# Where the value loads stand in the GpSimd queue of a fused attention and mixer kernel, and what its planner charges for them

## The chip, the cores and the metric

The kernel runs on one core of a Trainium2 chip. The metric is the time of one execution on the device, in microseconds (us). A core has these engines: TensorE (PE in the profile; its weight loads are PEld), VectorE (DVE), ScalarE (ACT), GpSimd (POOL) and SyncE (SP). SP and POOL also issue the DMAs of this kernel, each in its own queue and in program order; the profile calls the hardware queue of SP q1 and the software queue of POOL q0.

## What is computed

There are two stages: block-sparse attention (MoBA), then a token and channel mixer.

```
# attention: q, k, v are (4 batches, 8 heads, 768, 64)
k_rep = mean of k over blocks of 64 keys                  # 12 blocks
gate  = q @ k_rep^T, future blocks at -1e9
mask  = each query's top 3 blocks and its own block, and causal
x     = softmax(q @ k^T / 8, masked) @ v                  # heads side by side: (4, 768, 512)

# mixer
u   = x + (relu(x^T @ w_tok1) @ w_tok2)^T                 # 768 -> 256 -> 768
out = u + relu(u @ w_ch1) @ w_ch2                         # 512 -> 1536 -> 512
```

## The kernel before, in words

The 32 heads are handled as 16 pairs, i = 0 to 15, four pairs to a batch. The numbers below count pairs.

For each pair, `prepare(i)` (line 714) makes these pieces of work. SP loads k and q in float32 (`load_qk`, issued on line 313, two DMAs of 192 KB each for k and two for q). PE transposes them (line 358; tkl and tql in the profile), ACT copies the result out of PSUM to kt and qt (line 367), and POOL casts them to float16 into KA and QA (line 374; for pair 0 ACT does it, line 379). DVE sums keys by block (line 387), PE makes the gate scores (gps, line 405; for groups of pairs gtp, line 415), DVE picks the top three and builds the bias, PE transposes it (bps, line 493), and DVE puts it under QA (line 499). POOL loads the values (`load_v`, line 320) as float16 into one of six V buffers; pair i uses buffer i mod 6, so its load must come after the attention of pair i - 6.

`attend(i)` (line 791) then does for each head three score products (sps, line 513, with a triangle on line 517 for pair 0), three exponentials on ACT (line 526), the causal triangle on DVE (line 533), the product with V (avp, line 545), and the division on DVE (lines 553 and 564).

The mixer of a batch follows once its four pairs are done: tok (lines 576 and 607, with w_tok1), ups (lines 588 and 621, with w_tok2), and the two channel products c (line 657 with w_ch1 and line 678 with w_ch2). For batch 0 the token part is done one pair at a time (lines 607 and 621). Mixer work of one batch is put between the attention work of later ones. Small products on a zero tile, `dummy` (line 695), stand where PE has nothing else before 46 us of the plan.

The order is not written out by hand. Every piece of work is an `Op` with an engine, planned durations (`occ`, `rec`), a list of things it depends on (`deps`) and a priority. `plan` (line 109) simulates the engines at the time the program is built: again and again it takes the piece that can start first, and among those that can start within 60 ns the one with the lowest priority number. The program is then emitted in that order (lines 949 and 950), so that each engine has one fixed instruction order. What the chip waits for is decided apart from the plan, by the data that instructions share: an instruction waits only if it reads or overwrites something that another makes or still uses. An entry in `deps` with no data behind it moves a piece of work in the order and adds no wait on the chip.

Transfers are planned by `transfers` (line 80): one DMA stream for SP and one for POOL, each in order. A transfer begins 1250 ns (SP) or 1500 ns (POOL) after its issue (line 201), takes `size` ns at full rate, and its data counts as landed 700 ns (SP) or 1200 ns (POOL) later (line 105). While both streams are active, POOL gets the share of the rate that `SHARE` (line 77) names for the size of its transfer, and SP gets the rest. The sizes are 1750 for a k or q load of a pair (line 727), 1350 for a value load (line 752), 3200 for each of the two token weights and 2100 for each of the eight channel weights (line 838).

Two lists on lines 831 to 838 add dependencies by hand:

```python
for i in range(6):
    O["v", i].deps.append(O["tr", "ql", i])
...
for n, (at, f) in enumerate(wq):
    W.append(op("POOL", 700, 0, [O[("cast",) + WAIT[n]]], at, f, size=3200 if n < 2 else 2100))
```

So the value loads of pairs 0 to 5 are planned after the query transposes of their own pair (`tr ql`), those of later pairs only after the attention of pair i - 6, and each weight load after one of the casts named in `WAIT` (line 46). POOL's list begins with four copies of a constant (`indicator`, line 333).

Of the kernel before, what the change touches and what calls it, by code (L numbers as in the profile page):

```python
# [39 lines left out]
def QACT(i):  # L40
# [5 lines left out]
WAIT = [("kt", 3, 1), ("kt", 3, 1), ("qt", 3, 1), ("qt", 3, 1), ("qt", 4, 1), ("qt", 4, 1),  # L46
        ("qt", 5, 1), ("qt", 5, 1), ("qt", 6, 1), ("qt", 6, 1)]
# [26 lines left out]
QUEUES = ("SP", "ACTQ", "POOLQ")  # L74


SHARE = ((3000.0, 0.9), (2000.0, 0.9), (0.0, 0.65))


def transfers(moves):  # L80


    todo = {q: sorted([m for m in moves if (m[1].eng == "POOL") == q], key=lambda m: m[0]) for q in (True, False)}
    left = {id(o): o.size for _, o in moves}
    now, ends = 0.0, {}
    while todo[True] or todo[False]:
        head = {q: v[0] for q, v in todo.items() if v and v[0][0] <= now}
        if not head:
            now = min(v[0][0] for v in todo.values() if v)
            continue  # L90
        rate = {q: 1.0 for q in head}
        if len(head) == 2:
            big = head[True][1].size
            rate[True] = next(r for z, r in SHARE if big >= z)
            rate[False] = 1.0 - rate[True]
        step = min(left[id(o)] / rate[q] for q, (_, o) in head.items())
        for q, v in todo.items():
            if v and q not in head:
                step = min(step, v[0][0] - now)
        now += step  # L100
        for q, (_, o) in head.items():
            left[id(o)] -= step * rate[q]
            if left[id(o)] <= 1e-6:
                todo[q].pop(0)
                ends[o] = now + (1200 if q else 700)
    return ends


def plan(ops, rings, near=60.0):


    free = dict(PE=900.0, ACT=4800.0, DVE=4500.0, POOL=5200.0, SP=750.0, SPO=750.0)
    slots = {name: [(0.0, None)] * n for name, n in rings.items()}
    moves = []
    casts = []
    waiting = {}
    users = {}
    ready = {e: [] for e in free}
    done = {}
    for op in ops:  # L120
        n = 0
        for d in op.deps:
            users.setdefault(id(d), []).append(op)
            n += 1
        waiting[id(op)] = n
        if n == 0:
            ready[op.eng].append(op)

    def finish(op, eng):
        return done[id(op)] + (LAT.get(eng, 33) if op.size == 0 else 60)  # L130

    def buf_free(buf, eng):
        t = 0.0
        for u in buf.users:
            if id(u) not in done:
                return None
            t = max(t, finish(u, eng))
        return t

    order = []  # L140
    left = len(ops)
    while left:
        best = None
        for o in [o for o in ready["PE"] if o.prio == IDLE and free["PE"] > WARM_END]:
            ready["PE"].remove(o)
            done[id(o)] = free["PE"]
            left -= 1
        if not left:
            break
        for e, cand in ready.items():  # L150
            if not cand:
                continue
            lst = []
            if e == "SP":
                if any(x.eng == e and x.prio < min(c.prio for c in cand) for x in ops if id(x) not in done):
                    continue
                cand = [min(cand, key=lambda c: c.prio)]
            for op in cand:
                t = free[e]
                if op.prio == IDLE:  # L160
                    last = slots["av"][0][1]
                    f = 0.0 if last is None else buf_free(last, e)
                    if f is None or f > t:
                        continue
                for d in op.deps:
                    t = max(t, finish(d, e))
                ok = True
                for buf in op.takes:
                    first = None
                    for s, (_, old) in enumerate(slots[buf.ring]):  # L170
                        f = 0.0 if old is None else buf_free(old, e)
                        if f is not None and (first is None or f < first[0]):
                            first = (f, s)
                    if first is None:
                        ok = False
                        break
                    t = max(t, first[0])
                    buf.slot = first[1]
                if ok:
                    lst.append((t, op))  # L180
            if not lst:
                continue
            t0 = min(t for t, _ in lst)
            pick = min((x for x in lst if x[0] <= t0 + near), key=lambda x: (x[1].prio, x[0]))
            if best is None or pick[0] < best[0]:
                best = pick
        assert best is not None, "the plan cannot go on"
        t, op = best
        op.start = t
        for buf in op.takes:  # L190
            slots[buf.ring][buf.slot] = (0.0, buf)
        wait = 0.0
        if op.eng == "POOL" and not op.size:
            casts = [(t, t + op.rec)]
        elif op.two and casts and casts[0][0] <= t < casts[0][1]:
            wait = (casts[0][1] - t) % (450.0 if casts[0][1] - casts[0][0] > 900 else 1e9)
        free[op.eng] = t + op.occ + wait
        if op.eng in ("SP", "SPO"):
            free["SP"] = free["SPO"] = t + op.occ
        if op.size:  # L200
            moves.append((t + (1500 if op.eng == "POOL" else 1250), op))
            for o, d in transfers(moves).items():
                done[id(o)] = max(done.get(id(o), 0.0), d)
            now = min(free.values())
            moves = [(a, o) for a, o in moves if done[id(o)] > now - 2000]
        else:
            done[id(op)] = t + op.rec + wait
        ready[op.eng].remove(op)
        order.append(op)
        left -= 1  # L210
        for u in users.get(id(op), []):
            waiting[id(u)] -= 1
            if waiting[id(u)] == 0:
                ready[u.eng].append(u)
    return order, max(done.values())
# [3 lines left out]
def kernel(  # L219
# [71 lines left out]
    def op(eng, occ, rec, deps, prio, fn, takes=(), size=0):  # L291
        o = Op(eng, occ, rec, deps, prio, fn, takes, size)
        ops.append(o)
        return o
# [403 lines left out]
    O = {}  # L698
# [13 lines left out]
    W = []  # L712
# [115 lines left out]
        for i in G:  # L828
            attend(i)

    for i in range(6):
        O["v", i].deps.append(O["tr", "ql", i])
    own_op.deps.append(O["cast", "qt", 4, 1])
    for x in range(2):
        O["cast", "kt", 0, x].deps.append(O["qt", 0])
    O["ksum", 1].deps.append(O["bias", 0])
    for n, (at, f) in enumerate(wq):
        W.append(op("POOL", 700, 0, [O[("cast",) + WAIT[n]]], at, f, size=3200 if n < 2 else 2100))

    for b in range(B):  # L840
        fill = 1000.0 * (b + 1)
# [5 lines left out]
        if b == 0:  # L847
            for c in range(4):
                bk = Buf("bank")
                at = fill + c  # L850
# [64 lines left out]

    kernel_plan.update(ops=O)
    order, span = plan(ops, RINGS)


# [64 lines left out]
```

## Time and profile before

| what | value |
|---|---|
| median of 8 runs | 270.42 us (268.13 to 272.0) |
| the eight runs | 268.13, 268.33, 268.55, 270.11, 270.74, 270.83, 271.62, 272.0 us |
| profiled execution: own time / span | 271.62 us / 269.5 us |
| PE busy | 261.2 us, 97% of the span |
| DVE, ACT, POOL busy | 157.5, 145.3, 79.9 us |
| mean granted TensorE clock | 0.981 |
| DMA | 28.77 MB moved; q1 (SP) 21.33 MB, q0 (POOL) 7.08 MB |
| a value load, from issue to landing | 6.3 us median (4.0 to 9.5), x16 |
| a token weight load | 7.3 and 8.4 us |
| a k or q load (one DMA of 192 KB) | 5.5 and 5.4 us median, x32 each |

A value load keeps POOL for some 1.0 us while it is issued. The order on POOL in the first 60 us of the profiled execution, by start: value loads at 6.23, 8.17, 16.42, 31.39, 35.75, 39.95, 46.69, 49.40, 52.80 and 57.26 us; token weights at 32.39 and 33.20; pairs of channel weights at 36.79, 50.41 and 58.28; casts of pair 1 from 12.07, of pair 2 from 15.65, of pair 3 from 29.74 and of pair 4 from 45.03 us. By the dependencies above, the load at 35.75 belongs to pair 6 and the one at 39.95 to pair 7 (it waited for pair 1's attention), while those of pairs 4 and 5 are at 46.69 and 52.80.

How to read the table: PE is busy nearly always, but busy time includes the dummies and counts a slow product in full. Whether the time could be shorter is seen from what PE did and at which clock, stage by stage.

### The profile page before, as it was taken

Reading aid. Unit: us, or ns where it says so; the run is one execution under the profiler, and the core shown is the slowest. Engines: PE = TensorE matmul, PEld = TensorE weight load, DVE = VectorE, ACT = ScalarE, POOL = GpSimd, SP = SyncE. Lnnn points to the kernel's source line nnn. Section 1 sums busy time; section 2 is a strip of 40 time slices with the busy share of each in tenths; the row PEclk is TensorE's granted clock in tenths of the full one; section 3 lists DMA queues with packets and bytes.
Section 4 is the critical chain, followed back from the end, with each engine's and each line's share of the span. In section 5 each row is a group of like instructions: output and inputs, shape, how many; then the busy total and the mean of one; then the engine's idle time right before and its main releaser. Section 6 shows DMA issues by size and latency. Waiting matters only on the chain.

```text
span 269.5 us, 5879 instructions
## 1 busy us (share of the span) xinstructions
PE 261.2 (97%) x2322; PEld 170.4 (63%) x2322; DVE 157.5 (58%) x536; ACT 145.3 (54%) x195; POOL 79.9 (30%) x112
## 2 busy tenths in 40 slices
PE   7979999999999999899999999999999999999994
PEld 7967878878577768555655566655455544465443
DVE  4553686889696759987566976475233252333222
ACT  3753598877779985657883599860024400044100
POOL 8581563986742966026620000000000000000000
PEclk9985899999999999999999999999999999999999
DMA  8999699999999999119341000006320017210032
GB/s 171 191 204 219 135 157 201 173 184 197 217 179 146 208 172 125 25 56 168 55 83 43 14 2 2 0 2 124 148 78 2 0 23 174 88 68 0 2 133 100
DMA packets 91322, 28.77 MB, mean 107 GB/s; under 512 B 84896, under 2 KB 87840, under 8 KB 91296
## 3 DMA queue, kind: packets, MB, share of 16 engines
q1 hardware_dynamic: 63232, 21.33, 35.3%
q0 software_dynamic: 28064, 7.08, 27.0%
q8 instruction: 18, 0.29, 0.4%
q14 instruction: 8, 0.07, 0.1%
HBM read 26.83 MB, written 6.29 MB: 123 GB/s over the span
## 4 chain that ended last, share of the span: by engine, by line
PE 88%; DMA 5%; SPq 3%; DVE 1%; issue 1%; ACT 0%; DVEq 0%; ACTq 0%
PE c L657 23%; PE c L678 23%; PE sps L513 14%; PE avp L545 8%; DMA ql<-in_q_dram 5%; PE tql L358 3%; PE ups L588 3%; SPq L313 3%; PE tkl L358 3%; PE tok L576 2%; PE gps L405 2%; PE gtp L415 1%; PE avp L695 1%; PE bps L493 1%; PE tok L607 1%; PE ups L621 1%
## 5 line engine op out<-in xcount | busy, mean ns | idle before, releaser
L526 ACT ACTIVATE e<-sps 128x1024 f16<-128x1024 f32 (+1 forms) x96 | 84.6, 922 | 17.9 <-PE sps L513 11.6
L657 PE MATMUL c<-uT,wc 128*128 128x256 f16 (+1 forms) x384 | 69.1, 326 | 0.0
L678 PE MATMUL c<-wc,h 128*128 128x512 f16 (+2 forms) x300 | 65.6, 371 | 0.0
L667 ACT ACTIVATE h<-c 128x512 f16<-128x512 f32 x48 | 28.8, 600 | 61.7 <-PE c L657 42.5
L513 PE MATMUL sps<-QA,KA 88*128 88x512 f16 (+3 forms) x256 | 51.4, 312 | 0.8 <-ACT e L526 0.7
L657 PEld LDWEIGHTS <-wc 128*128 128x128 f16 x384 | 36.5, 97 | 23.3 <-issue 0.2
L678 PEld LDWEIGHTS <-h 128*128 128x128 f16 x300 | 28.6, 97 | 30.6 <-issue 0.8
L533 DVE TENSOR_TENSOR e<-e,m 128x256 f16<-128x256 f16 x90 | 27.6, 314 | 20.5 <-ACT e L526 19.9
L374 POOL CAST KA<-kt 64x768 f16<-64x768 f32 x30 | 24.7, 822 | 46.5 <-ACT kt L367 29.4
L669 DVE TENSOR_SCALAR h<-c 128x256 f16<-128x256 f32 x48 | 20.3, 422 | 26.0 <-PE c L657 25.7
L686 DVE TENSOR_TENSOR ob<-u,c 128x512 f32<-128x512 f16 (+2 forms) x25 | 16.5, 664 | 32.1 <-PE c L678 32.1
L513 PEld LDWEIGHTS <-KA 88*128 88x128 f16 x256 | 23.4, 101 | 18.4 <-issue 3.1
L545 PEld LDWEIGHTS <-e 128*128 128x128 f16 x672 | 25.9, 99 | 2.8 <-issue 0.2
L545 PE MATMUL avp<-V,e 128*128 128x65 f16 x672 | 27.1, 195 | 0.0
L374 POOL CAST QA<-qt 64x768 f16<-64x768 f32 x30 | 25.7, 855 | 2.6 <-ACT qt L367 1.3
L387 DVE TENSOR_REDUCE kst<-kt 128x12 f32<-128x768 f32 x16 | 15.2, 948 | 6.5 <-ACT kt L367 6.2
L367 ACT COPY kt<-tkl 128x768 f32<-128x768 f32 x16 | 12.8, 798 | 11.4 <-PE tkl L358 8.2
L320 POOL DMA_DIRECT2D V<-in_v_dram x16 | 16.5, 1030 | 7.5 <-PE sps L513 4.3
L564 DVE TENSOR_TENSOR x<-avp,rc 128x384 f16<-128x384 f32 x32 | 17.8, 555 | 0.8
L367 ACT COPY qt<-tql 128x768 f32<-128x768 f32 x16 | 12.8, 802 | 8.0 <-PE tql L358 7.9
L499 DVE COPY QA<-bps 24x640 f16<-24x640 f16 x32 | 14.3, 481 | 2.6 <-PE bps L493 2.3
L358 PE MATMUL tql<-id,ql 128*128 128x128 f32 x96 | 13.4, 276 | 2.2 <-DMA ql<-in_q_dram 2.2
(66 smaller groups left out, 222.0 us busy)
## 6 DMA issues: line engine op xcount, KB each, us to landing
kl<-in_k_dram SPq DMA_DIRECT2D x32, 192.0 KB, 5.5
ql<-in_q_dram SPq DMA_DIRECT2D x32, 192.0 KB, 5.4
out_dram<-ob SPq DMA_DIRECT2D x23, 256.0 KB, 2.0
V<-in_v_dram POOLq DMA_DIRECT2D x16, 192.0 KB, 6.3
wc<-in_moe_w_ch_dram POOLq DMA_DIRECT2D x8, 384.0 KB, 8.1
w<-in_moe_w_tok_dram POOLq DMA_DIRECT2D x2, 384.0 KB, 7.8
out_dram<-ob SPq DMA_DIRECT2D x1, 160.0 KB, 1.8
out_dram<-ob SPq DMA_DIRECT2D x1, 96.0 KB, 1.7
```

The lines of the kernel that those rows point to most:

```text
L358: nc.tensor.transpose(out=p[:, 128 * j:128 * j + 128], in_=t[:, j, :], identity=ident32)
L367: nc.scalar.copy(out=t, in_=p[:, 0:S])
L374: nc.gpsimd.tensor_copy(out=to, in_=src)
L513: nc.tensor.matmul(out=p[:, off + a:off + a + n], lhsT=KA[i % R][x][0:MK, 128 * kk:128 * kk + 128], rhs=QA[i % R][x][0:MK, q0 + a:q0 + a + ...
L526: nc.scalar.activation(out=e[:, 0:width], in_=T["sps", i, x, g][:, 0:width], func=AF.Exp, scale=scale)
L533: nc.vector.tensor_tensor(out=d, in0=d, in1=m0.rearrange("p (a b) -> p a b", a=1).broadcast_to([128, 2, 128]), op=ALU.mult)
L545: nc.tensor.matmul(out=p[:, jq, :], lhsT=T["e", i, x, g][:, o:o + 128], rhs=V16[i % (R + 1)][:, x, kk, :], start=(kk == 0), stop=(kk == jq))
L564: nc.vector.tensor_tensor(out=T["x16", b][:, :, 64 * hh:64 * hh + 64], in0=T["aps", i, x][:, :, 0:64], in1=T["rc", i, x].broadcast_to([128 ...
L657: nc.tensor.matmul(out=p, lhsT=wc1_16[:, cc, 128 * fc:128 * fc + 128], rhs=T["uT", b][:, cc, a // 128:e // 128, :], start=(cc == 0), stop= ...
L667: nc.scalar.activation(out=T["h2", b][:, fc, a:e], in_=T["c1", b, fc, n], func=AF.Relu)
L669: nc.vector.tensor_scalar(out=T["h2", b][:, fc, a:e], in0=T["c1", b, fc, n], scalar1=0.0, scalar2=None, op0=ALU.max)
L678: nc.tensor.matmul(out=T["c2", b, j, lo], lhsT=T["h2", b][:, fc, 128 * j:128 * j + 128], rhs=wc2_16[:, fc, lo:hi], start=(fc == 0), stop=( ...
```

## The change

```diff
-SHARE = ((3000.0, 0.9), (2000.0, 0.9), (0.0, 0.65))
+SHARE = ((3000.0, 0.8), (2000.0, 0.9), (0.0, 0.6))
...
-            moves.append((t + (1500 if op.eng == "POOL" else 1250), op))
+            moves.append((t + (1900 if op.eng == "POOL" else 1250), op))
...
-    for i in range(6):
-        O["v", i].deps.append(O["tr", "ql", i])
+    for i, d in enumerate((1, 2, 2, 3, 3, 4, 4, 5, 6, 7, 8, 9, 10, 11, 12, 13)):
+        O["v", i].deps.append(O["tr", "ql", d])
...
-        W.append(op("POOL", 700, 0, [O[("cast",) + WAIT[n]]], at, f, size=3200 if n < 2 else 2100))
+        W.append(op("POOL", 700, 0, [O[("cast",) + WAIT[n]]], at, f, size=4500 if n < 2 else 2100))
```

Four numbers or lists change, all of them inputs of the planner. In the plan, the value load of pair 0 now comes after the query transposes of pair 1, that of pair 1 after those of pair 2, pairs 2 and 3 after their own, pair 4 after those of pair 3, pair 5 after those of pair 4, pairs 6 and 7 after those of pairs 4 and 5, pairs 8 to 15 after those of pair i - 2. A transfer of POOL is planned to begin 400 ns later than before; while SP transfers too, a token weight has 0.8 of the rate in place of 0.9 and a value load 0.6 in place of 0.65; a token weight counts as 4500 ns of transfer in place of 3200. No instruction is added, removed or changed in itself; the order of instructions on every engine may change, since the plan is made anew.

## The prediction

> **What bounds the kernel now.** I read the 40 slices first: where PE is full, and at which clock.
>
> ```profile
> PE   7979999999999999899999999999999999999994
> ...
> PEclk9985899999999999999999999999999999999999
> DMA  8999699999999999119341000006320017210032
> ```
>
> A slice is 6.74 us. From the fifth slice on PE is full at full clock; slices 3 to 5 (13.5 to 33.7 us) show granted clocks of 8, 5 and 8 tenths. So whatever comes after some 50 us is a fixed amount of PE work done without gaps, and a microsecond won or lost ahead of it reaches the end as it is. The stage to read is the front. Its windows (start:end, length, then PE, PEld, DVE, ACT and POOL busy with counts, the clock, DMA share, GB/s):
>
> ```profile
> 16.00:17.00 1.00, 0.16 (x2) 0.06 (x1) 0.98 (x4) 0.00 (x0) 1.00 (x2) 1.00 1.08 219
> 17.00:18.00 1.00, 0.53 (x5) 0.56 (x6) 0.94 (x11) 0.00 (x0) 0.95 (x2) 1.00 1.05 209
> 18.00:19.00 1.00, 1.00 (x9) 0.70 (x8) 0.72 (x2) 0.65 (x1) 0.30 (x1) 0.71 1.21 205
> 19.00:20.00 1.00, 1.00 (x13) 1.00 (x12) 0.00 (x0) 0.94 (x2) 0.79 (x1) 0.50 2.08 167
> ...
> 26.00:28.00 2.00, 2.00 (x27) 2.00 (x26) 0.46 (x2) 1.13 (x2) 0.00 (x0) 0.50 0.99 184
> ...
> 29.00:30.00 1.00, 1.00 (x18) 0.78 (x15) 0.79 (x2) 0.96 (x2) 0.26 (x1) 1.00 0.05 12
> ```
>
> PE and ACT stand still together from 16.2 to 17.5 us; at about 18.3 us the clock falls to half, and it is back at about 28.6. The timeline of that place names the cause (start, duration, engine, line, what; in brackets the idle time before it):
>
> ```profile
> 6.23 1.18 POOL L320 DMA_DIRECT2D V<-in_v_dram  x1
> ...
> 8.17 1.01 POOL L320 DMA_DIRECT2D V<-in_v_dram  x1
> ...
> 8.56 3.11 SPq L313 DMA_DIRECT2D ql<-in_q_dram  x2
> ...
> 12.07 1.70 POOL L374 CAST KA<-kt 64x768 f16<-64x768 f32 x2 [2.89 <-ACT kt L367]
> ...
> 13.86 0.85 PE L358 MATMUL tkl<-id,kl 128*128 128x128 f32 x6 [0.37 <-DMA kl<-in_k_dram]
> ...
> 14.91 1.25 PE L405 MATMUL gps<-ks,qt 128*128 128x24 f32 x10
> ...
> 17.47 0.85 PE L358 MATMUL tql<-id,ql 128*128 128x128 f32 x6 [1.31 <-DMA ql<-in_q_dram]
> ...
> 18.36 0.80 ACT L367 COPY qt<-tql 128x768 f32<-128x768 f32 x1 [2.77 <-PE tql L358]
> ```
>
> PE's order has pair 2's query transposes next, and the load is late. The chain of waits agrees (start, length):
>
> ```profile
> 9.45 7.88 DMA ql<-in_q_dram
> ...
> 17.47 0.85 PE tql L358 x6
> ```
>
> That load took 7.88 us against a median of 5.4 us for its line. Both value loads, of pairs 0 and 1, were in flight beside it: issued at 6.23 and 8.17, landed 7.2 and 7.9 us later (at 13.4 and 16.1). Note the first row: pair 0's value load, planned after pair 0's query transposes, was issued at 6.23, while those transposes began at 6.60. The planned dependency holds nothing on the chip; only the place in POOL's order counts.
>
> **The change part by part.** Its sum is made against the profiled execution: 271.62 us, of which 269.5 is the span and 2.1 lies around it. It is one of the longest of the eight runs (median 270.42; three lie at 268.13 to 268.55).
>
> Value loads of pairs 0 and 1. I follow the planner's rules by hand for order alone. Without a value load in the way, SP's fourth load of 1750 ns (pair 1's q) is planned to land at 10.1 us and its transposes to be done at 11.2. The four constant copies on POOL are planned to end at 8.6 us, pair 1's casts to begin at 11.8. So pair 0's load moves from before the fourth copy to after it. Its issue on the chip moves from 6.23 to about 7.1 (the copy takes 0.84). Pair 1's load now follows pair 2's query transposes, planned to be done after 14.6 us, and stands behind both casts of KA and QA of pair 1, probably also behind one of pair 2: on the chip from 8.17 to some 15.6 to 16.5 us, where pair 2's load is now (16.42). What is moved past what: the copy and three to five casts on POOL go earlier by 1.0 each in the queue, but pair 1's casts waited 2.89 us for kt anyway, so that gains nothing; pair 2's second KA cast and its QA casts (17.48 and 19.21) come up to 1.0 later, and their reader, the scores of pair 2, starts after pair 2's bias is put (29.21) and at PE's turn at 31 us or later. That cover is 8 us or more; without it the cost would be 1.0. Pair 1's values, issued at 16.5 and landed at most 9.5 us later (the longest of 16), are there at 26; their first reader, the second pair's product with V, runs at 36.43. Pair 0's are there some 7.2 us after 7.1, at 14.3; their reader runs at 26.11.
>
> What it buys: pair 2's q load then has one value load beside it. Bounds from the rows: 5.4 us (median of its line) to 7.88 (nothing won). About 390 KB less to read at the 209 GB/s of that window is 1.9 us, so I take 6.0, landing at 15.4. PE is busy with gps until 16.16, so the wait of 1.31 is gone whole; of the 0.37 at 13.86 I take half. Next late is PE's own order: gps, then the transposes, without a gap. ACT's wait of 2.77 for qt shrinks by as much, and the exponentials behind it move up. Together -1.5 us (bounds 0 and -1.68).
>
> The clock. It was at half from 18.3 to 28.6. In the 5 us windows 15 to 20, 20 to 25 and 25 to 30 the granted clock was 0.84, 0.50 and 0.63: 0.8 + 2.5 + 1.85 = 5.15 us of full clock lost. Some 14 dummies lie inside (12 at 18.97, 2 at 24.84); at half clock they take about 1.5 us, half of it lost in nothing needed, so at most 4.4 us of need. Below, the bound is 0: ACT may pace the scores. The three shortest runs, mean 268.34, are 3.3 us under the profiled one, and I read them as runs without this fall, though only one profile is there to see. I take -3.1. The fall came 0.8 us after PE's only idle stretch over a microsecond. If that stretch closes, scores follow the transposes at once.
>
> A rule that speaks against this step stands in the Trainium skill, "TensorE: Matmul & The Clock Gate", Part 1 and the table at the end: the clock goes to half after an idle window of about 3.4 us, windows run freely, and gaps above some 3 us are what to avoid. The longest gap here was 1.31 us, and the clock fell all the same. By the rule a gap of 1.31 is harmless and closing it leaves the clock as it is, so the sum would be 270.5; by the row it is 267.4. The same page's Part 4 says that transposes count less as activity, which would reconcile the two.
>
> Value loads of pairs 4 to 15. Pairs 4 and 5 are brought forward (46.69 to about 36, 52.80 to about 47), pairs 6 and 7 go back (35.75 to about 47, 39.95 to about 53), pairs 8 and 9 go from 49.40 and 57.26 to behind the transposes at 62.86 and 65.23. Each is still ahead of its reader. POOL also loses the 2.05 us it stood at 39.95. Cost: two transfers of 1.9 us are moved behind 58 us. The k and q loads there have room: pair 8's k is issued at 52.85 and read at 76.0. The last q load, landing 5.97 us after its issue at 104.31, made PE wait 0.61 at 110.37; one more value load beside it could cost 1.9. Bounds -0.6 and +1.9; I take +0.1, since the nearest value load there, at 102.18, stays: it waits for pair 7's attention.
>
> Weights. The charge for a token weight grows by 400 ns of start and from 3200 / 0.9 = 3556 to 4500 / 0.8 = 5625 ns beside SP: 2.47 us in the plan, so tok of batch 0 (39.77, 41.98, 48.00) is placed up to 2.47 us later among PE's work. The chip's loads are unchanged: issued at 32.39, landed 7.3 to 8.4 later, at 39.7 to 40.8, just when tok began. So the later place is either a saved wait in executions where the weight is late (up to -1.1) or filler that is missing (up to +2.47, since after the dummies end PE has nothing else). PE lost only 0.41 at 38.4 there and ACT was busy 4.69 of 5 us from 40 to 45, so scores cannot all come forward; I take +0.3. Shares and the 400 ns for value loads shift planned landings by less than 1 us, and no reader is within 8 us: nothing.
>
> Sum: 271.62 - 1.5 - 3.1 + 0.1 + 0.3 = 267.4 us, 1.1% under the median.
>
> **The rivals.** B, the clock falls all the same: for it speaks that 14.9 to 18.2 us hold gate products, transposes and a pause of 1.31, so that closing the pause puts only more of the same there; against it, the place of the fall. 271.62 - 1.5 + 0.4 = 270.5.
>
> C, the value load does not move, or the gap moves with it: if pair 1's load is still planned ahead of its casts it is issued at about 8.2 again, or pair 2's transposes are put before the gate in PE's order and PE waits there. Against it, 14.6 in the plan lies well behind 11.8. Nothing changes: 270.4.
>
> D, the slower end: the filler is late. If tok and ups of batch 0 move back by the full charge of 2.47 us and nothing takes their place at 40 to 48 us, the profiled time becomes 271.62 + 2.47 = 274.1 without a gain at the front. For it: ACT nearly full there, and no dummies after 46 us of the plan. Against it: PE already has the transposes of pairs 4 and 5 at hand. It decides from some 1.5 us of gap on, which is 273.1 and 1% over the median.
>
> **How the numbers follow.** The likeliest, A, has 0.56 and its own range is 265.5 (all of 1.68 and 4.4) to 268.9 (ACT paces part of it). B has 0.18, C 0.11, D 0.15. About 1% is what a measurement of this kernel can tell from no change: 267.7 and 273.1. Of A some 0.43 lies under 267.7, which is "faster"; the rest of A with B, C and a little of D (0.01) makes "same", 0.43; "slower" is the rest of D, 0.14. The range goes from A's low end to 271.8, which holds A, B and C with the spread of the runs shown and leaves out D.
>
> **What would show it.** Right: the second value load on POOL behind pair 1's casts, at 15 us or later; no wait of PE for ql near 16 us; clock at 10 tenths in slices 3 to 5; pair 3's key transposes (27.28 before) at 24 or earlier. Wrong: a clock that falls without a gap (B), a wait that reappears at tql or tkl (C), dummies or idle time between 39 and 50 us above the 0.3 us of now (D), or a longer wait near 110 us.

## The result and the profile after

The changed kernel takes 266.91 us (median of 11 runs, 265.17 to 268.62) against 269.82 us before (32 runs): ratio 0.9907, 95% interval 0.9879 to 0.9935. Its profiled execution took 266.91 us with a span of 264.8 us; the one of before 271.62 and 269.5. The ratios here and below leave out the longest executions of each kernel (of the 86 of before that stand beside the experiments, 19, of which 17 have a mean clock of 0.987 or less, so they are mostly those with the longest stretches at half clock), while medians, and counts of executions by their clock, hold all of them.

The slices of the changed kernel (page, part 2; a slice is now 6.62 us):

```profile
PE   8989999999999999999999999999999999999994
...
PEclk9997999999999999999999999999999999999999
DMA  8999999999999999168511000009220025310032
```

Three slices below full clock (8, 5, 8) have become one (7). The windows of the same stretch:

```profile
16.00:17.00 1.00, 1.00 (x12) 1.00 (x10) 0.63 (x3) 0.92 (x2) 1.00 (x2) 1.00 0.89 147
17.00:18.00 1.00, 1.00 (x11) 0.81 (x11) 0.60 (x6) 0.21 (x2) 0.96 (x2) 1.00 1.16 202
18.00:19.00 1.00, 1.00 (x10) 0.91 (x10) 0.86 (x10) 0.94 (x1) 0.94 (x2) 1.00 1.14 93
19.00:20.00 1.00, 0.66 (x9) 0.45 (x7) 0.90 (x2) 0.60 (x1) 0.94 (x2) 0.93 1.65 159
20.00:22.00 2.00, 2.00 (x12) 1.13 (x11) 1.90 (x14) 0.58 (x2) 1.22 (x2) 0.50 1.99 163
...
23.50:24.00 0.50, 0.50 (x11) 0.50 (x8) 0.26 (x2) 0.32 (x1) 0.00 (x0) 1.00 1.16 256
```

From 16 to 18 us, where PE and ACT stood still, PE is full and ACT at work. The clock still falls, at about 19.9 us, but is back at about 23.3: 3.4 us in place of 10.2 (18.4 to 28.6). The timeline shows why the pause is gone (start, duration, engine, line, what):

```profile
7.00 1.18 POOL L320 DMA_DIRECT2D V<-in_v_dram  x1
...
8.61 1.73 SPq L313 DMA_DIRECT2D ql<-in_q_dram  x2
...
13.60 0.85 PE L358 MATMUL tkl<-id,kl 128*128 128x128 f32 x6 [0.80 <-DMA kl<-in_k_dram]
...
15.47 0.83 PE L358 MATMUL tql<-id,ql 128*128 128x128 f32 x6
15.75 2.02 POOL L320 DMA_DIRECT2D V<-in_v_dram  x2
16.14 1.19 PE L405 MATMUL gps<-ks,qt 128*128 128x24 f32 x10
```

Pair 0's value load went from 6.23 to 7.00 us, pair 1's from 8.17 to 15.75, right ahead of pair 2's. Pair 2's query transposes ran at 15.47 in place of 17.47 and waited for nothing. SP's own issue of that load became shorter too, 1.73 us against 3.11. What is left in front is a wait of 0.80 us for pair 2's k load, which has pair 0's value load beside it.

### The profile page after: what moved, and what is told of

Same layout as the page of the kernel before. It is cut to its first block, busy times and chain, and to the rows that moved or that the text cites. A ratio compares the mean times of both kernels' runs of the same rounds, so it can differ in the third digit from the quotient of the medians.

```text
span 264.8 us, 5842 instructions
## 1 busy us (share of the span) xinstructions
PE 257.5 (97%) x2304; PEld 167.6 (63%) x2304; DVE 158.6 (60%) x536; ACT 145.3 (55%) x195; POOL 79.9 (30%) x112
## 4 chain that ended last, share of the span: by engine, by line
PE 84%; DVE 7%; SPq 2%; DMA 2%; ACT 2%; issue 1%; POOL 0%; DVEq 0%; ACTq 0%
PE c L657 23%; PE c L678 23%; PE sps L513 13%; PE avp L545 7%; PE ups L588 3%; PE tql L358 3%; PE tkl L358 2%; DMA kl<-in_k_dram 2%; SPq L313 2%; PE tok L576 2%; DVE m L463 1%; DVE kst L387 1%; PE gtp L415 1%; DVE QA L499 1%; PE gps L405 1%; ACT e L526 1%
## 5 line engine op out<-in xcount | busy, mean ns | idle before, releaser
L678 PEld LDWEIGHTS <-h 128*128 128x128 f16 x300 | 28.6, 97 | 30.6 <-issue 1.0
L533 DVE TENSOR_TENSOR e<-e,m 128x256 f16<-128x256 f16 x90 | 29.6, 337 | 14.9 <-ACT e L526 14.1
L686 DVE TENSOR_TENSOR ob<-u,c 128x512 f32<-128x512 f16 (+2 forms) x25 | 16.5, 664 | 32.2 <-PE c L678 32.1
L513 PEld LDWEIGHTS <-KA 88*128 88x128 f16 x256 | 23.3, 100 | 17.6 <-issue 1.5
L320 POOL DMA_DIRECT2D V<-in_v_dram x16 | 16.5, 1032 | 5.6 <-PE avp L545 3.4
L358 PE MATMUL tkl<-id,kl 128*128 128x128 f32 x96 | 14.2, 287 | 0.8 <-DMA kl<-in_k_dram 0.8
```

Source lines behind the costliest of these rows:

```text
L358: nc.tensor.transpose(out=p[:, 128 * j:128 * j + 128], in_=t[:, j, :], identity=ident32)
L513: nc.tensor.matmul(out=p[:, off + a:off + a + n], lhsT=KA[i % R][x][0:MK, 128 * kk:128 * kk + 128], rhs=QA[i % R][x][0:MK, q0 + a:q0 + a + ...
L533: nc.vector.tensor_tensor(out=d, in0=d, in1=m0.rearrange("p (a b) -> p a b", a=1).broadcast_to([128, 2, 128]), op=ALU.mult)
L678: nc.tensor.matmul(out=T["c2", b, j, lo], lhsT=T["h2", b][:, fc, 128 * j:128 * j + 128], rhs=wc2_16[:, fc, lo:hi], start=(fc == 0), stop=( ...
```

## The experiments

Two kinds of edit are used. Some plan anew. The others plan as one of the two kernels does and then move single instructions in the finished order, so that every other instruction keeps its place; they use this helper behind the call of `plan`:

```python
    def move(o, after):
        order.remove(o)
        order.insert(order.index(after) + 1, o)
```

Ratios are to before, with 95% intervals. "Clock kept" counts the executions whose mean granted clock was 0.9975 or more, that is, with next to no stretch at half clock; before has 30 of 86 over the three sets of its runs beside these experiments, the changed kernel 6 of 12 (one execution more than its median above holds).

### e1: only the two front value loads moved

```diff
+    move(O["v", 0], ind_op[4])
+    move(O["v", 1], O["cast", "qt", 1, 1])
```

> The order of before on every engine, with only the value loads of pairs 0 and 1 put elsewhere in POOL's order: pair 0's behind the fourth constant copy, pair 1's behind pair 1's second QA cast, as in the changed kernel. Theory FRONT (the gain comes from pair 1's value load leaving the way of pair 2's q load): ql of pair 2 lands by about 15.5 us, no PE wait of 1.3 us at its transposes, the half clock is gone or short, and the time is 0.988 to 0.993 of before, all of the change's 0.9907. Rival REPLAN (the gain comes from the new order of the other engines and the later loads): the ql wait goes but the time stays at 0.997 to 1.003.

Ratio 0.9886 (0.9820 to 0.9951), 266.92 us, clock kept in 4 of 6. Windows of its front (start:end, length, PE busy, and further on the clock):

```profile
15.00:20.00 5.00, 5.00 (x54) 4.35 (x54) 3.76 (x27) 2.74 (x4) 4.79 (x6) 1.00 1.44 193
20.00:25.00 5.00, 5.00 (x86) 4.38 (x84) 4.43 (x13) 4.01 (x6) 2.45 (x4) 1.00 1.51 198
```

Before, the same two windows have PE at 3.69 and 5.00 us and the clock at 0.84 and 0.50. Two loads moved, with nothing else changed, give a gain that can't be told from that of the whole change; with six executions the interval reaches 0.9951, so that half of it isn't excluded. FRONT holds; for a gain of this kind REPLAN isn't needed.

### e2: the changed kernel with the two loads put back

```diff
+    move(O["v", 0], ind_op[3])
+    move(O["v", 1], ind_op[4])
```

> The order of the changed kernel on every engine, with only the value loads of pairs 0 and 1 back where before has them (behind the third and the fourth constant copy). FRONT: PE waits again for the k or q load of pair 2 (1 us or more), the clock falls for longer, and the ratio to before is 0.998 to 1.005. REPLAN: the wait comes back but the ratio stays at 0.989 to 0.993.

Ratio 0.9963 (0.9910 to 1.0015), clock kept in 3 of 12. Its PE waits (engine, line, waited for: us in total, times, longest):

```profile
PE tql L358 <- DMA ql<-in_q_dram: 2.0, 1, 2.0
...
PE tkl L358 <- DMA kl<-in_k_dram: 1.2, 1, 1.2
```

The wait is back, larger than before's 1.31, the profiled clock is at half for 6.8 us, and most of the gain is gone. The ratio lies a little under what FRONT expected (0.998); its interval holds 1.0 and also a remainder of some tenths of a per cent, while the medians, 269.72 against 269.95 us, are 0.1% apart. The three executions that kept the clock took 266.8 us, 1.5 less than those of before that kept it. Whether the load was late in these three isn't known, since the profiled execution is another; but the rest of the change seems to be worth something too.

### e3 and e4: the dependencies alone, and the charges alone

```diff
# e3, from before; e4 is the changed kernel with these lines the other way round
-    for i in range(6):
-        O["v", i].deps.append(O["tr", "ql", i])
+    for i, d in enumerate((1, 2, 2, 3, 3, 4, 4, 5, 6, 7, 8, 9, 10, 11, 12, 13)):
+        O["v", i].deps.append(O["tr", "ql", d])
```

> Before with the new list of dependencies of the value loads alone, all charges old; planned anew. FRONT: the same two loads move, so 0.988 to 0.994. Rival CHARGES (the new charges of the POOL queue bring the gain): 0.997 to 1.005.

> The changed kernel with the old dependencies of the value loads: only the shares, the 1900 ns and the 4500 ns are new. FRONT: pair 1's value load is issued near 8 us again, pair 2's q load is late, and the ratio is 0.997 to 1.01. CHARGES: 0.989 to 0.994.

e3: 0.9988 (0.9943 to 1.0034), clock kept in 4 of 12. e4: 0.9971 (0.9921 to 1.0020), clock kept in 7 of 12. Neither half shows the gain. For e4 this is as FRONT says: pair 1's value load is issued at 8.18 us again. For e3 FRONT failed: its front is that of the changed kernel (value loads at 7.01 and 15.97, PE busy 4.65 us from 15 to 20), yet the time is that of before. The loss is further on, in e3's timeline at pair 15's transposes, and in its windows after them:

```profile
106.84 0.85 PE L358 MATMUL tkl<-id,kl 128*128 128x128 f32 x6 [1.62 <-DMA kl<-in_k_dram]
108.30 0.98 PE L358 MATMUL tql<-id,ql 128*128 128x128 f32 x6 [0.60 <-DMA ql<-in_q_dram]
```

```profile
108.00:110.00 2.00, 1.71 (x9) 1.11 (x10) 1.91 (x6) 0.68 (x1) 0.00 (x0) 0.72 0.00 0
110.00:112.00 2.00, 2.00 (x6) 0.67 (x5) 0.65 (x1) 0.24 (x2) 0.00 (x0) 0.50 0.00 0
```

PE waits 2.2 us for pair 15's loads and the clock falls a second time. In the timeline, two value loads (96.45 and 98.57 us) stand just ahead of those loads (98.99 and 100.05); in the changed kernel they are at 93.52 and 97.92. There the later of pair 15's two k DMAs landed after 5.6 us against 7.3 in e3, so that the key transposes ran at 104.51 without a wait, and its query transposes come later in PE's order.

### e5: the pause filled, the late load left

```diff
+    at = order.index(O["tr", "ql", 2])
+    order[at:at] = [Op("PE", 54, 54, [], IDLE, dummy(n)) for n in range(20)]
```

> Before, order and loads untouched, with 20 more products on the zero tile (about 54 ns each, 1.1 us in all) put where PE waits for pair 2's q load. It takes the idle stretch away and leaves the late load. Theory CLOCK (the fall of the clock follows from the idle stretch of 1.3 us and is the larger part of the gain): the granted clock stays at 0.998 or more in nearly every execution and the time is 0.992 to 0.996 of before. Rival ACTIVITY (gate products and transposes, not the idle stretch, bring the fall, and the gain is the wait itself): the clock is spread as before, 0.981 to 1.0, and the ratio is 0.998 to 1.003.

Ratio 0.9980 (0.9952 to 1.0007), median 268.69 against 269.68; clock kept in 9 of 12. The load was as late as ever:

```profile
15.80 1.23 PE L695 MATMUL avp<-warm 128*128 128x122 f16 x20
18.07 0.85 PE L358 MATMUL tql<-id,ql 128*128 128x128 f32 x6 [1.04 <-DMA ql<-in_q_dram]
```

```profile
15.00:20.00 5.00, 3.96 (x53) 3.62 (x52) 3.18 (x16) 1.43 (x3) 3.34 (x5) 1.00 1.28 179
20.00:25.00 5.00, 5.00 (x67) 4.07 (x65) 3.30 (x17) 3.59 (x5) 1.46 (x2) 1.00 1.15 201
```

Each theory has one half right. With products that nothing needs put into the wait, the clock stays more often (9 of 12, against 10 of 28 executions of before in the same set). It isn't shown that the pause as such decides: the load came later still, 1.04 us of pause is left in this profile, and the clock stayed; it also stayed in the profiles of e4, e11 and e12, which have pauses of 0.9 to 1.2 us there. And this is not the larger part of the gain: 1.0 us in the medians, 0.2% in the ratio, which its interval doesn't tell from nothing.

### e6: e3 with the late value loads moved away

```diff
+    move(O["v", 13], O["cast", "qt", 12, 1])
+    move(O["v", 12], O["cast", "qt", 12, 1])
```

> The kernel with the new dependencies alone (e3), with only the value loads of pairs 12 and 13 moved in POOL's order, from before pair 12's casts to behind them, out of the way of pair 15's k and q loads. Theory GIVEN BACK (that kernel wins the front as the changed one does and loses it again at 107 us, where PE waited 2.2 us for pair 15's k and q and the clock fell to half): no wait there, no second fall, and the ratio is 0.987 to 0.994. Rival ORDER (the old charges cost it elsewhere): the wait goes and the ratio stays at 0.996 to 1.002.

Ratio 0.9971 (0.9937 to 1.0006), median 268.99 against e3's 270.14; clock kept in 6 of 12. PE waits for no load at 107 us, and its pauses from 100 to 120 us fall from 2.23 to 0.73 us. So the two value loads were what made pair 15 late. Yet GIVEN BACK explains only a part. PE still has 1.08 us of pauses between 50 and 75 us, where the changed kernel has 0.23: waits for DVE and ACT (0.4 and 0.5 us at 53 and 57 us). They belong to the order which the old charge of a token weight makes, for e12 below, which keeps that charge, has the same two waits at 54 and 58 us, and e11 has not.

### e7: pair 0's value load later too

```diff
+    move(O["v", 0], O["cast", "kt", 1, 1])      # in the changed kernel
```

> The changed kernel with pair 0's value load moved too, from behind the constant copies (7.0 us) to behind pair 1's two KA casts (about 14 us). FRONT in double dose: pair 2's k load lands 1 us earlier, PE's wait of 0.8 us before its key transposes goes, and the ratio to before is 0.985 to 0.990, if the load of 7 us still lands before pair 0's product with V (22.5 us). Rival SATURATED (k and q are no longer what PE waits for): the wait goes and the ratio stays at 0.989 to 0.993.

Ratio 0.9860 (0.9819 to 0.9901), 265.74 us, clock kept in 5 of 6. Pair 2's k no longer keeps PE waiting (its q now does, 0.44 us at 15.40), the value load (14.28) lands in time for its product with V at 20.85, and pair 3's key transposes run at 21.51 (23.54 in the changed kernel, 27.28 before). A part comes back as a new wait, 1.36 us for a k load at 82 us, where the changed kernel begins the same transposes at 82.55 without a wait. The loads issued between 52 and 66 us are not slower than there (11.7 to 13.3 us from issue to landing, against 12.0 to 13.6 from 50 to 66), but SP comes to this k load 3.3 us later, at 71.88 in place of 68.59, held by the issue of the q load ahead of it (6.44 us in place of 3.85). First e7:

```profile
65.34 6.44 SPq L313 DMA_DIRECT2D ql<-in_q_dram  x2
...
71.88 4.14 SPq L313 DMA_DIRECT2D kl<-in_k_dram  x2
...
82.34 0.85 PE L358 MATMUL tkl<-id,kl 128*128 128x128 f32 x6 [1.36 <-DMA kl<-in_k_dram]
```

Then the changed kernel:

```profile
64.64 3.85 SPq L313 DMA_DIRECT2D ql<-in_q_dram  x2
...
68.59 7.09 SPq L313 DMA_DIRECT2D kl<-in_k_dram  x2
...
82.55 0.85 PE L358 MATMUL tkl<-id,kl 128*128 128x128 f32 x6
```

### e8: the changed kernel with its pauses filled

```diff
+    for o, n in ((O["tr", "kl", 2], 12), (O["mask", 1], 6)):
+        at = order.index(o)
+        order[at:at] = [Op("PE", 54, 54, [], IDLE, dummy(m)) for m in range(n)]
```

> The changed kernel with products on the zero tile put where PE waits: 12 ahead of pair 2's key transposes (a wait of 0.8 us) and 6 ahead of pair 1's mask transposes (0.34 us). CLOCK: the remaining stretch at half clock (19.7 to 23.4 us in the profile) goes in nearly all executions, and the ratio is 0.984 to 0.989. ACTIVITY: the clock falls as often as in the changed kernel and the ratio stays at 0.989 to 0.994.

Ratio 0.9924 (0.9892 to 0.9957); clock kept in 9 of 11. The clock stays more often, as CLOCK says (9 of 11 against 6 of 12 would be too few to show it alone; e5 points the same way), and the time is no better than the changed kernel's. The two waits themselves are not gone: 0.47 us for pair 2's k load and 0.55 at the mask transposes are left. Executions that kept the clock took 266.76 us on average, the changed kernel's 266.13, and in the profile PE now waits 1.2 us for a q load at 85 us, where it waited 0.5 us for ACT in the changed kernel. What was won in front was probably given back there:

```profile
85.02 0.85 PE L358 MATMUL tql<-id,ql 128*128 128x128 f32 x6 [1.23 <-DMA ql<-in_q_dram]
```

### e9 and e10: the second channel weight loaded later

```diff
+    move(W[6], O["cast", "qt", 8, 1])
+    move(W[7], W[6])
+    move(W[8], O["cast", "qt", 9, 1])
+    move(W[9], W[8])
```

e10 is the changed kernel with these lines; e9 has the line of e7 as well.

> The changed kernel with pair 0's value load behind pair 1's KA casts (as e7) and the four loads of the second channel weight, which stood between 50 and 62 us, moved behind the casts of pairs 8 and 9 (two near 75 us, two near 86 us); their first reader stands near 103 us. Theory MIDDLE FULL (what holds e7 back from the whole gain of the front is the DMA between 45 and 75 us, where its k and q loads take 10 to 13 us and PE waits 1.4 us for a k load at 82): that wait goes, and the ratio to before is 0.979 to 0.984. Rival NO ROOM (the weight lands late, or k and q are late elsewhere): a PE wait for a load between 85 and 112 us, and 0.985 to 0.992.

> The changed kernel with only those four weight loads moved. Its PE waited for no load between 50 and 120 us. MIDDLE FULL matters only when the front runs ahead: so the ratio stays where the changed kernel is, 0.988 to 0.993, and what it gains over that tells how much of the 0.5 us idle time at 85 us was a load. Rival: 0.985 or less, if the back pressure on SP's queue set the changed kernel's pace in the middle.

e9: 0.9857 (0.9823 to 0.9890), 265.28 us, the fastest here, clock kept in 6 of 6. e10: 0.9949 (0.9914 to 0.9985), clock kept in 6 of 12, no gain over the changed kernel and perhaps a small loss. MIDDLE FULL is half right: in e9 the k and q loads issued from 55 to 66 us land after 4.6 to 7.5 us in place of 11.7 to 13.3, the wait at 82 us is gone and PE has no pause from 50 to 75 us, but other waits came, as NO ROOM said:

```profile
100.22 0.84 PE L358 MATMUL tql<-id,ql 128*128 128x128 f32 x6 [0.72 <-DMA ql<-in_q_dram]
103.30 0.84 PE L358 MATMUL tkl<-id,kl 128*128 128x128 f32 x6 [0.67 <-DMA kl<-in_k_dram]
```

The second two of the moved weight loads are now issued at 83.62 us, among the k and q loads that SP issues for the last pairs from 82.85 us on. e9 and e7 can't be told apart; the intervals of e9 and of the changed kernel overlap (0.9823 to 0.9890, 0.9879 to 0.9935), so that e9 is likely, not surely, the faster of the two.

### e11 and e12: which charge the dependencies need

```diff
# e11: before with the new dependencies and
-size=3200 if n < 2
+size=4500 if n < 2
# e12: before with the new dependencies and
-SHARE = ((3000.0, 0.9), (2000.0, 0.9), (0.0, 0.65))
+SHARE = ((3000.0, 0.8), (2000.0, 0.9), (0.0, 0.6))
...
-            moves.append((t + (1500 if op.eng == "POOL" else 1250), op))
+            moves.append((t + (1900 if op.eng == "POOL" else 1250), op))
```

> The new dependencies with one of the new charges, 4500 for a token weight; shares and the 1500 ns are old. The dependencies alone (e3) won the front and lost it at 107 us and at 53 to 57 us. Theory SIZE (the later place of the token products of batch 0 is what keeps the middle free of waits): 0.988 to 0.994, like the changed kernel. Rival RATE (the 400 ns and the shares do it): 0.996 to 1.002, like the dependencies alone.

> The new dependencies with the other two charges, the 1900 ns and the shares; a token weight still counts 3200. SIZE: 0.996 to 1.002. RATE: 0.988 to 0.994. If both this and the run with the size alone end between, the charges act only together.

e11: 0.9931 (0.9892 to 0.9970), clock kept in 4 of 12. e12: 0.9984 (0.9949 to 1.0020), clock kept in 5 of 12. SIZE: with 4500 alone the kernel is near the changed one, with the other two charges it is where the dependencies alone are. In e12's profile PE waits for the token weight itself:

```profile
36.77 0.84 PE L607 MATMUL tok<-x,w 128*128 128x128 f16 x12 [1.12 <-DMA w<-in_moe_w_tok_dram]
```

e11 has no such wait, and PE has no pause at all between 30 and 50 us (1.12 in e12) and 0.23 us from 50 to 75 (1.07 in e12). The intervals of e11 and e12 still touch, so this rests on the trace as much as on the times.

## Why the prediction was right, and where it was not

The forecast was 267.4 us, faster by 1.1% of the median, in a range of 265.5 to 271.8; measured were 266.91 us and 0.93%. The place and the mechanism at the front were right. The clock's term was mis-sized, that of the weights had the wrong sign, and that the sum came out so close is in part luck.

**The planned dependency holds nothing on the chip.** Right, and it gave the places: pair 0's load at 7.00 (7.1 forecast), pair 1's at 15.75 (15.6 to 16.5). The step that looked most uncertain, reading the order from the planner's rules by hand, held.

**Pair 2's q load.** Right: no wait at its transposes, pair 3's key transposes at 23.54 (24 or earlier). One sign of being wrong came in part: PE's wait for pair 2's k load grew from 0.37 to 0.80, where half of it should have gone. PE's busy time less the dummies was 4.92 us from 10 to 20 us before and 6.59 after, 1.67 more (1.5 forecast), though busy time counts a slow product in full. Two runs with the order of before and the clock kept measure the term better: 267.2 us with the load in time (e1, 4 executions) and 268.6 with it late (e5, 9), 1.4 us apart. Executions that kept the clock took 268.3 us before (30 of them) and 266.1 after (6): 2.2 us that no clock explains, of which -1.5 and +0.4 left only 1.1. In e1, which has only the two front loads moved, the same difference is 1.1; so about half of the 2.2 is the front, and the other half comes with the new order behind it. These are few executions, and some tenths are chance.

**The clock.** That the stretch around the wait decides is right as far as e5 tests it: more products there, and the clock falls less often. That the pause as such brings the fall isn't shown, and rival B (the fall stays) was right in part: the clock still falls in half the executions, for a shorter time, so that slice 4 reads 7 tenths where full clock was forecast. In the profile it falls at 19.9 us with only 0.34 us of pause next to it, behind 2.4 us of gate products between 16.14 and 18.96. That second cause was not isolated. The size, -3.1, was wrong. To read the three shortest runs (mean 268.34) as runs without the fall was right, for those that kept the clock average 268.33. But the term took a profiled execution with 10.2 us at half clock for the usual one, while the median execution of before had less: of 269.82 - 266.91 = 2.9 us, 2.2 is there at full clock too, which leaves 0.7 to the clock; the products of e5 alone gave 1.0. The error nearly vanished because the sum began at the same execution, 1.8 us above the median: start and term were too large together. That is luck, and the +0.4 for the rest of the change, where the runs have some -1.1, erred the other way. The rule of the Trainium skill, "TensorE: Matmul & The Clock Gate", that gaps above some 3 us are to be avoided, did not predict these falls: the longest pause near them was 1.31 us before and 0.34 after.

**Late value loads.** The bound of +1.9 was needed, the +0.1 was right only for this combination. The wait of 0.61 us for a load at 110 us is gone in the changed kernel (PE pauses there 0.52 us for DVE instead), but with the dependencies alone the same kind of wait grew to 2.2 us, and the clock fell with it (e3). So the premise that a microsecond won ahead of 50 us reaches the end as it is does not hold in general. That loads further on can pay back the front is what my sum treated as a tail; it decides e3 and holds back e7, e9 and probably e8.

**Weights.** The step that failed is "filler that is missing", +0.3, with rival D and its 274.1 behind it. The runs show the other end that I had bounded at -1.1. The token products of batch 0 moved from 39.77 to 37.38 us in the profiled executions, and did not wait: the weight itself is issued earlier (27.98 against 32.39) and lands 9.2 us later, at 37.2, and PE had no pause from 30 to 50 us. Where the old size stands in an order with an early front, PE waits for that weight: 0.92 us in e1, 0.79 in e5, 1.12 in e12. In e6 and e3, whose profiled fronts lost time to a fall of the clock, the wait is 0.16 and nothing. With the size alone the dependencies gain (e11), without it they don't (e12). I had seen that the weight landed just when its product began (the first one, at 39.7; the second, issued at 33.20, landed at 41.6 and not at 40.8, and nothing waited for it), and yet priced the later place as a loss.

What stays open: how much of e6's remaining distance to the changed kernel is the order in 50 to 75 us and how much is chance of the clock, what the change is worth behind the front to better than some tenths of a us, and what makes the clock fall at 19.9 us.

## What to carry to other kernels

Where a planner writes the order, find which of its inputs become waits on the chip and which only move instructions; then test a move by moving that one instruction in the finished order, since planning anew changes everything else and can hide the gain (e1 against e3). A load that nothing needs for another 28 us (8.17 to 36.43 for pair 1's values before) can cost time by standing beside one that is needed now, and a charge in the plan is worth comparing with the measured landing time of its load: here raising that of the token weights helped (e11), and raising the others showed no gain (e12). When a front gets faster, look for the next place where the loads are late: here most gains in front met one between 82 and 107 us.

## What the runs showed of the hardware

The granted clock came in steps. In the traces every fall to half clock lasted 3.41 us or a whole multiple of it, read from the clock in windows of 0.2 us: 3.41 in the changed kernel, twice in e3, in e6 and in e10, 6.83 in e2, and 10.24 before. One such step is 0.0064 of a mean clock over 265 us, and most mean clocks of an execution lie near 1.0, 0.994, 0.987 or 0.981. Over 86 executions of the same kernel before, time followed those steps, from 268.3 us at full clock to some 272 us at 0.981. Products that feed nothing kept the clock more often (e5: 9 of 12 against 30 of 86, 10 of 28 in its own set). Landing times of k and q loads stretched from a median of 5.5 us to over 13 us between 44 and 66 us of e7 and of the changed kernel, while the DMA row of the slices read 9 tenths there as it does through nearly all of the first 100 us; that row doesn't tell how late a load will be.
